# GEGLU feed-forward on one core: x's second half transposed in four places, stored by two transfers behind w_down's loads; the 21 staging steps spread anew; T3's second half later

## The chip, the cores and the metric

One core of one Trainium2 chip runs the kernel. The metric is the device time of one execution in microseconds (us); the time shown for a kernel is the median over several runs. Engines are named as the profile names them: PE is TensorE (matmuls; PEld are its weight loads), DVE is VectorE, ACT is ScalarE, POOL is GpSimd, and SPq and ACTq are the queues in which SyncE and ScalarE issue DMAs. Each engine and each queue works in the order of its program, so an instruction that waits holds everything behind it.

## The reference

With x of 2048 x 1024, w_gate and w_up of 1024 x 3584 and w_down of 3584 x 1024, all in bfloat16:

```python
def reference(x, w_gate, w_up, w_down):
    return (_gelu(x @ w_gate) * (x @ w_up)) @ w_down      # _gelu: tanh form
```

## The kernel before

**Seven products in place of eight.** Every matrix product is cut into 2 x 2 blocks and done with the seven products m1 to m7 of the Strassen-Winograd scheme. It needs sums of blocks on both sides. For the first two matmuls the sums of weights are s1 to s4 and a22 (`s_sum`: s1, s2, s4 on POOL, s3 on DVE in the stage in question (`s3_both`, L490), a22 on ACT), and the sums of the transposed x are t1, t2, t3, b22 and t4 (`t_sum`, L300 on DVE, b22 on ACT). For the third matmul the left sums come from the hidden activations (`s_down`, L763, DVE), and the right sums T1 to T4 from w_down. T2 and T4 of w_down are the same for all four output groups, so they are made once, early, and kept in DRAM (`t_dram`).

**Order of the work.** The 2048 rows of x are two halves `h` of 1024. For each half the kernel makes the hidden activations `hT` (28 tiles of 128 features by 1024 rows, "pairs" of tiles at a time), then multiplies by w_down in two groups (`down_group`). For h = 0 the sequence of pairs is: `first_units` (plain products of eight tiles, and the sums t1 to t4), the two pairs MID (4, 5), the eight pairs LEADS (0, 1, 2, 3, 6, 7, 8, 9), then two ordinary groups of two pairs, (10, 11) and (12, 13). For one pair, `quads` issues the products in the order m6/m5, then m7, m3, m4, each for gate (j = 0) and up (j = 1), of four matmuls each: 40 matmuls a pair. MID and the ordinary groups issue 32 plain matmuls ahead of their two pairs; LEADS do not, since theirs come from `first_units`. Between the products, DVE adds (`add_m5`, L527: PSUM bank plus the saved m5), ACT copies and applies the gelu (L313), and DVE multiplies gelu by up into hT (`mult`, L318). The third product m3 reads the bank that the first add writes, so PE waits for that add.

**Hooks.** The lists `thens` name, for each pair, what is issued at a point of its sequence: "start" (before its products), "m5" (after the first two adds), "m7", "m3" and "m4" (after those products), and "m1" (between the plain products of a group). All is put on engines and queues in this written order: `on` chains the instructions of each engine.

**Staging of w_down's sums.** `stage_load` (L701) loads two rows of blocks of w_down into one of three `wd_sb` buffers. `stage_step(n)` (L718 on DVE, 128 x 1024), n from 0 to 20, works in threes: the first makes a difference in a buffer of `o_sb`, the second subtracts it from another block in place and stores the buffer to `t_dram` (L721, 512 KB), the third makes the other sum in the other `o_sb` buffer and stores that as well. There are two such buffers, so a step that begins a buffer anew must wait until the last store from it has landed. `run_steps(n)` issues the next n steps; `run_loads` issues the loads that have become due. `run_late` issues one `s_down` "s3" on DVE. For the down phase itself, `load_wd_rows` (L633) fetches the first eight row blocks of w_down by two loads of 1 MB, issued on SPq at the m7 of pair 11; the buffers of pair 11's weights must be free by then.

**x's second half.** For h = 1 the transposed x is fetched in two parts. Its second 512 rows go into the buffer `xT1` by eight DMA transposes on SPq (`stage_x` with tb = 1, L214), two at the start of each of the third to sixth LEADS pairs. Its first 512 rows have no buffer yet: eight DMA transposes (L737) put them into tiles 24 to 27 of hT, which hold weights of chunk (0, 4) until the last LEADS pair's sums are made and get their activations in group (12, 13). `store_x` (L742) moves them from there to `x_dram`, and `x_fill` (L1125) loads them back in the down phase.

```python
        def run_x():
            m = 2 if xs[:1] and xs[0][0] == 1 else 4
            for q in xs[:m]:
                stage_x(hT, *q)
            del xs[:m]
```

Of the kernel before, what the change touches and what calls it, by code (L numbers as in the profile page):

```python
# [34 lines left out]
def kernel(  # L35
# [8 lines left out]
    nc = tc.nc  # L44
# [5 lines left out]
    KD = D // P  # L50
    KH = KD // 2
# [78 lines left out]
    def sp(inst):  # L130
        return on("sp", inst)
# [88 lines left out]
    def new_x(tb):  # L220
        xT[tb] = xT_pool.tile([P, KD, TB], BF16, name=f"xT{tb}")
# [147 lines left out]
    def first_units(hT):  # L369

        gs = {}

        def gelus(held, tiles):
            for u, t in enumerate(tiles):
                gs[t] = gelu(banks[held[u][0]])

        def outs(held, tiles):
            for u, t in enumerate(tiles):
                mult(hT, gs[t], banks[held[u][1]], t, 0)

        sets = ((VB, RB), (QB, PB), (QB, PB), (VB, RB))

        def top(n, j, k0, k1):
            tiles = (2 * n, 2 * n + 1)
            plain_products(sets[n], tiles, j, k0, k1)
            if k1 == KH:
                hold(sets[n], tiles, j)

        def rest(n):
            tiles = (2 * n, 2 * n + 1)  # L390
            plain_products(sets[n], tiles, 0, KH, KD)
            gelus(sets[n], tiles)
            plain_products(sets[n], tiles, 1, KH, KD)
            return sets[n], tiles

        transpose_x0(0)
        warm(RB[1], TB // 2)
        top(0, 0, 0, KPQ)
        top(0, 1, 0, KPQ)
        transpose_x0(1)  # L400
        top(1, 0, 0, KPQ)
        top(0, 0, KPQ, KH)
        top(0, 1, KPQ, KH)
        top(1, 1, 0, KPQ)
        top(1, 0, KPQ, KH)
        top(1, 1, KPQ, KH)
        outs(*rest(1))
        outs(*rest(0))
        for j in range(2):
            top(2, j, 0, KH)  # L410
        for j in range(2):
            top(3, j, 0, KH)
        t_sum("t1", 0, KH // 2)
        t_sum("t1", KH // 2, KH)
        t_sum("t2")
        outs(*rest(2))
        t_sum("t3", 0, KH // 2)
        t_sum("t3", KH // 2, KH)
        t_sum("b22")
        outs(*rest(3))  # L420
        t_sum("t4", 0, KH // 2)
        t_sum("t4", KH // 2, KH)
        for j in range(2):
            s_sum(0, MID[0], j, "s3")
        for j in range(2):
            for name in ("s1", "s2"):
                s_sum(0, MID[0], j, name)
        for j in range(2):
            s_sum(0, MID[0], j, "s4")
# [291 lines left out]
            sp(nc.sync.dma_start(out=dst, in_=t.bitcast(F32)))  # L721


    staged_x = []

    def x_rows(k0, k1):
        return x_dram[k0:k1, :, :].rearrange("k p t -> p k t")

    def stage_x(hT, tb, kd):
        if tb == 1:  # L730
            load_xT(xT, 1, tb, kd, kd + 1)
            return
        c0 = kd % NTB * TB
        f0 = KF - KD // NTB + kd // NTB
        t = hT[:, f0 : f0 + 1, c0 : c0 + TB]
        src = xv[SH : SH + TB, kd : kd + 1, :]
        sp(nc.sync.dma_start_transpose(out=t, in_=src))  # L737
        staged_x.append((x_rows(kd, kd + 1), t))

    def store_x():  # L740
        for dst, src in staged_x:
            sp(nc.sync.dma_start(out=dst, in_=src))  # L742
        staged_x.clear()

    def s_down(hT, grp, name, i0, i1):
        n = 0 if name in ("s1", "s2", "s4") else 1
# [223 lines left out]
    for h in range(NH):  # L970
# [33 lines left out]
                stage_load(loads.pop(0))  # L1004

        def run_x():
            m = 2 if xs[:1] and xs[0][0] == 1 else 4
            for q in xs[:m]:
                stage_x(hT, *q)
            del xs[:m]  # L1010

        if h == 0:
            run_loads()

            def load_half(c, f0):
                if f0 == 0:
                    new_chunk((0, c))
                for j in range(2):
                    load_w((0, c), j, 0, KD, act, f0, f0 + FA)

            thens = [
                {
                    "start": [
                        lambda j=j: s_sum(0, MID[0], j, "a22") for j in range(2)
                    ],
                    "m5": [lambda: load_half(3, 0)],
                    "m3": [lambda: run_steps(1)],
                    "m4": [lambda: new_x(1), run_loads],
                },
                {  # L1030
                    "m5": [lambda: load_half(3, FA)],
                    "m7": [lambda: fetch_to(QB, 0)],
                    "m3": [lambda: run_steps(1), run_loads],
                },
            ]
            quads(hT, h, MID, (h, LEADS[0]), thens, False, True, True)
            thens = [{} for _ in LEADS]
            for n in range(NL):
                thens[n]["start"] = []
                thens[n]["m3"] = [lambda: run_steps(1), run_loads]  # L1040
            for n in range(NL // 2):
                thens[2 + n]["start"].append(run_x)
            thens[1]["start"].append(lambda: load_half(4, 0))
            thens[3]["start"].append(lambda: load_half(4, FA))
            thens[5]["start"].append(lambda: load_half(5, 0))
            thens[5]["m7"] = [lambda: load_chunk((0, 6))]
            thens[7]["start"] += [lambda: load_half(5, FA), run_x]
            thens[7]["m3"].append(run_x)
            thens[7]["m4"] = [store_x]
            quads(hT, h, LEADS, (h, begin), thens, True, False, True)  # L1050
            s_late.append(
                shared_pool.tile([P, NL // 2 * TB], F32R, name="s_late")
            )
            run_late()

        for lead in range(begin, NPAIR, PPG):
            members = range(lead, lead + PPG)
            thens = [{} for _ in members]

            def add(n, name, *fs):  # L1060
                thens[n].setdefault(name, []).extend(fs)

            add(1, "m3", lambda key=(h, lead // PPG + 2): load_chunk(key))
            if h == 0:
                add(0, "m1", lambda: run_steps(2), run_loads)
                few = lead == NPAIR - PPG
                add(0, "start", lambda: run_steps(2), run_loads)
                for n in range(1 if few else PPG):
                    add(n, "m3", lambda: run_steps(1), run_loads)
                    add(n, "m4", run_late)  # L1070
            for n, pair in enumerate(members):
                if pair == NPAIR - 2 - (h == 0):
                    add(
                        n,
                        "start" if h else "m7",
                        lambda: load_wd_rows(0, 4),
                        lambda: load_wd_rows(4, 8),
                    )
                if h > 0 and 6 < pair < 11:
                    i = s3_late[pair - 7]  # L1080
                    at = "start" if n == 0 else "m3"
                    add(n, at, lambda i=i: s_down(hT, 0, "s3", i, i + 2))
                if pair < NPAIR - 1:
                    continue
                add(
                    0,
                    "m1",
                    lambda: early.append(wd_pool.tile([P, WDT, D], BF16, name="wd_sb")),
                    lambda: s_down(hT, 0, "s3", 0, 4),
                )  # L1090
                add(
                    n,
                    "start",
                    lambda: load_b22(4, NS),
                    lambda: load_wd_rows(8, 10),
                    lambda: load_wd_rows(10, 12),
                    lambda: load_wd_rows(12, NS),
                    lambda: load_b22(0, 4),
                )
                add(n, "m6", lambda: t_down(0, "t1", 4, 6))  # L1100
                add(n, "m7", lambda: s_down(hT, 0, "s1", 4, 8))
                add(n, "m7", lambda: s_down(hT, 0, "s1", 0, 4))
                add(n, "m3", lambda: t_down(0, "t1", 0, 2))
                add(
                    n,
                    "m4",
                    lambda: t_down(0, "t2", 0, NT2),
                    lambda: t_down(0, "t1", 2, 4),
                    lambda: t_down(0, "t1", 6, 8),
                    lambda: s_down(hT, 0, "s1", 8, NS),  # L1110
                    lambda: t_down(0, "t1", 8, NS),
                )
            nxt = (h, lead + PPG) if lead + PPG < NPAIR else None
            quads(hT, h, members, nxt, thens, lead == 0)
# [78 lines left out]
```

## Time and profile before

| what | value |
|---|---|
| median of 3 runs (range) | 548.77 us (548.61 to 550.17) |
| the profiled execution's own time | 549.52 us |
| its span, first to last instruction | 547.7 us |
| mean granted TensorE clock | 0.994 |
| PE busy | 535.0 us, 98% of the span |
| DVE busy | 379.9 us, 69% |
| ACT busy | 274.0 us, 50% |
| POOL busy | 254.9 us, 47% |
| moved by DMA | 102.70 MB, 188 GB/s on average |

The page gives busy time by engine, the span in 40 slices, the chain of work that ended last, groups of instructions by line, and DMA issues. A busy PE says little alone: matmuls are pipelined and their ends are modelled, so what counts is where PE stood idle and at which granted clock it ran. Where a time of day is given below, it counts from the start of the span.

### The profile page before, as it was taken

The page shows a single profiled execution, that of the slowest core. Times are in us where ns is not written, and L with a number is a line of the kernel's source. Part 1 is how long each engine was busy: PE and PEld are TensorE (multiplying, and loading weights), DVE is VectorE, ACT ScalarE, POOL GpSimd, SP SyncE. Part 2 cuts the span into 40 slices and gives each one's busy share as a digit, 9 for nine tenths or more (in the row PEclk, how much of TensorE's full clock was granted, in tenths as well). Part 3 has the DMA queues.
Part 4 walks back from the last instruction along what each step waited for, and adds up shares of the span by engine and source line. Part 5 has one row for each costly group of instructions (what it writes and reads, how often), then busy time and mean ns, then how long its engine had stood idle before and what let it go on. Part 6 is the DMA issues. An engine that isn't in the chain of part 4 may idle for free.

```text
span 547.7 us, 7014 instructions
## 1 busy us (share of the span) xinstructions
PE 535.0 (98%) x2380; PEld 383.8 (70%) x2380; DVE 379.9 (69%) x467; ACT 274.0 (50%) x471; POOL 254.9 (47%) x202
## 2 busy tenths in 40 slices
PE   9999999999599999999999999999999999999997
PEld 4448888886376767768668686867767686866866
DVE  1496899999479999789574352535444659979951
ACT  4456666665245416414565555555565552462270
POOL 0098999997546800000025594949586770000000
PEclk9999999999979999999999999999999999999999
DMA  8964357599766596969980404133140419677846
GB/s 235 264 229 117 115 177 170 161 262 222 240 193 230 186 350 231 332 204 328 298 278 0 154 1 156 32 122 92 62 152 3 153 60 330 230 251 245 287 145 204
DMA packets 97844, 102.70 MB, mean 188 GB/s; under 512 B 18320, under 2 KB 72720, under 8 KB 97808
## 3 DMA queue, kind: packets, MB, share of 16 engines
q1 hardware_dynamic: 71344, 82.52, 48.1%
q10 hardware_dynamic: 26464, 19.73, 12.0%
q8 instruction: 19, 0.31, 0.2%
q14 instruction: 17, 0.14, 0.1%
HBM read 85.98 MB, written 12.58 MB: 180 GB/s over the span
## 4 chain that ended last, share of the span: by engine, by line
PE 95%; DVE 2%; issue 1%; SPq 1%; DMA 1%; ACT 0%; DVEq 0%
PE bank L511 57%; PE bank L791 32%; PE bank L355 5%; DVE o_sb L718 1%; DVE hT L318 1%; SPq L742 1%; PE bank L245 1%; DMA t_dram<-o_sb 1%; PE bank L337 0%; DVE bank L527 0%; SPq L737 0%; ACT o_sb L847 0%; DVEq L718 0%; DVE wd_sb L763 0%; DVEq L318 0%
## 5 line engine op out<-in xcount | busy, mean ns | idle before, releaser
L511 PE MATMUL bank<-t_mem,s_mem 128*128 128x512 f32 x1096 | 254.6, 393 | 7.3 <-DVE bank L527 7.3
L511 PEld LDWEIGHTS bank<-t_mem,s_mem 128*128 128x128 f32 x1096 | 207.0, 189 | 52.2 <-issue 8.3
L462 POOL TENSOR_TENSOR s_mem<-w_mem 128x512 fp32r<-128x512 bf16 x80 | 101.0, 1281 | 186.0 <-DVE t_mem L300 94.8
L318 DVE TENSOR_TENSOR hT<-w_mem,bank 128x512 bf16<-128x512 f32 x106 | 71.1, 684 | 68.9 <-PE bank L511 40.3
L527 DVE TENSOR_TENSOR bank<-bank,m 128x512 f32<-128x512 f32 x112 | 72.3, 693 | 47.3 <-ACT m L567 45.1
L791 PE MATMUL bank<-t_mem,s_mem 128*128 128x512 f32 x416 | 98.1, 393 | 0.0
L313 ACT ACTIVATE w_mem<-bank 128x512 f32<-128x512 f32 x106 | 62.7, 597 | 65.8 <-DVE bank L527 44.6
L791 PEld LDWEIGHTS bank<-t_mem,s_mem 128*128 128x128 f32 x416 | 78.1, 188 | 17.1
L511 PE MATMUL bank<-xT,w_mem 128*128 128x512 bf16 x320 | 71.1, 379 | 0.9 <-DVE hT L318 0.9
L462 POOL TENSOR_TENSOR s_mem<-w_mem,s_mem 128x512 fp32r<-128x512 bf16 x46 | 65.1, 1434 | 7.9 <-PE bank L511 7.9
L690 DVE TENSOR_TENSOR t_mem<-w_mem 128x1024 fp32r<-128x1024 bf16 x56 | 66.7, 1240 | 0.4 <-PE bank L511 0.4
L511 PEld LDWEIGHTS <-w_mem 128*128 128x128 bf16 x320 | 30.6, 98 | 39.2 <-issue 3.8
L462 POOL TENSOR_TENSOR s_mem<-s_mem,w_mem 128x512 fp32r<-128x512 f32 x46 | 54.7, 1208 | 0.2
L572 ACT COPY bank<-bank 128x512 f32<-128x512 f32 x56 | 32.0, 572 | 23.3 <-PE bank L511 19.7
L567 ACT COPY m<-bank 128x512 f32<-128x512 f32 x56 | 33.0, 589 | 19.2 <-PE bank L511 19.1
L475 ACT CAST s_mem<-w_mem 128x512 fp32r<-128x512 bf16 x48 | 29.5, 616 | 25.6 <-PE bank L511 24.4
L791 PEld LDWEIGHTS <-hT 128*128 128x128 bf16 x224 | 21.3, 98 | 26.6 <-issue 2.1
L856 ACT CAST o_sb<-bank 128x512 bf16<-128x512 f32 x27 | 14.9, 586 | 33.7 <-PE bank L791 33.7
L791 PE MATMUL bank<-t_mem,s_late 128*128 128x512 f32 (+1 forms) x132 | 30.3, 382 | 0.0
L537 ACT COPY bank<-bank 128x512 f32<-128x512 f32 x40 | 22.8, 570 | 13.2 <-PE bank L511 13.2
L763 DVE TENSOR_TENSOR s_mem<-hT 128x512 fp32r<-128x512 bf16 x36 | 23.6, 688 | 6.4 <-PE bank L791 6.4
L791 PEld LDWEIGHTS bank<-t_mem,s_late 128*128 128x128 f32 x132 | 24.4, 188 | 4.9
(61 smaller groups left out, 400.8 us busy)
## 6 DMA issues: line engine op xcount, KB each, us to landing
t_mem<-t_dram SPq DMA_DIRECT2D x56, 512.0 KB, 5.2
wd_sb<-in_w_down_dram SPq DMA_DIRECT2D x26, 512.0 KB, 6.9
t_dram<-o_sb SPq DMA_DIRECT2D x14, 512.0 KB, 3.3
w_mem<-in_w_gate_dram ACTq DMA_DIRECT2D x6, 1024.0 KB, 5.8
w_mem<-in_w_up_dram ACTq DMA_DIRECT2D x6, 1024.0 KB, 8.2
w_mem<-in_w_gate_dram SPq DMA_DIRECT2D x8, 512.0 KB, 6.1
w_mem<-in_w_up_dram SPq DMA_DIRECT2D x8, 512.0 KB, 7.1
w_mem<-in_w_down_dram SPq DMA_DIRECT2D x4, 1024.0 KB, 7.2
```

The source lines that it names most:

```text
L313: act(nc.scalar.activation(out=g_sb, in_=ps[:], func=ACT.Gelu_apprx_tanh))
L318: nc.vector.tensor_tensor(out=hT[:, fc, tb * TB : (tb + 1) * TB], in0=g_sb, in1=ps[:], op=ALU.mult,)
L355: nc.tensor.matmul(banks[held[u][j]][:], lhsT=w_sb[:, kd, f0 : f0 + P], rhs=xT[0][:, kd, :], start=kd == 0, stop=kd in (KH - 1, KD - 1), s ...
L462: pool(nc.gpsimd.tensor_tensor(out=t, in0=in0, in1=in1, op=op))
L475: act(nc.scalar.copy(out=t, in_=a(1, 1)))
L511: nc.tensor.matmul(banks[bank][:], lhsT=lhs[:, c, :], rhs=rhs[:, c, :], start=start and c == 0, stop=c == KH - 1, skip_group_check=True,)
L527: nc.vector.tensor_tensor(out=banks[dst][:], in0=banks[src][:], in1=m5[:], op=ALU.add)
L567: act(nc.scalar.copy(out=m5[j][:], in_=banks[V_[j]][:]))
L572: act(nc.scalar.copy(out=banks[R_[j]][:], in_=banks[Q_[j]][:]))
L690: dve(nc.vector.tensor_tensor(out=t, in0=in0, in1=in1, op=ALU.subtract))
L763: dve(nc.vector.tensor_tensor(out=t, in0=in0, in1=in1, op=op))
L791: nc.tensor.matmul(banks[bank][:, c0:c1], lhsT=lhs(i, u), rhs=rhs(i)[:, c0:c1], start=start and i == 0, stop=stop and i == NS - 1, skip_gr ...
```

## The change

Five things change; the matmuls, the sums and every value computed stay the same.

1. In `first_units`, the second half of t3 is issued on DVE behind the multiplications of the last plain unit and behind b22, instead of ahead of them.
2. The 21 staging steps are spread anew. Before: one step at the m3 of each MID pair and of each LEADS pair (steps 0 to 9), then six in group (10, 11) and five in group (12, 13): two at "m1", two at "start", one at the m3 of each pair but the very last. Now: the first MID pair takes three (start, m3, m4), the second one; LEADS take one each, the last of them at its m4 instead of its m3; the two groups take two at "m1", one at "start" and one at each m3, as long as there are any (steps 12 to 16 and 17 to 20).
3. The eight transposes into hT, before four at the start and four at the m3 of the last LEADS pair, are issued two at its start, two at its m7, two at its m3 and two at its m4.
4. `store_x`, before eight stores of 128 KB at the m4 of the last LEADS pair, becomes two stores of 512 KB: one at the m5 of pair 10, one at its m3, each behind a load of w_down in SPq.
5. One more `run_late` at the m4 of pair 10, so that the late "s3" sums end sooner.

```diff
         t_sum("t3", 0, KH // 2)
-        t_sum("t3", KH // 2, KH)
         t_sum("b22")
         outs(*rest(3))
+        t_sum("t3", KH // 2, KH)
...
-        staged_x.append((x_rows(kd, kd + 1), t))
-
-    def store_x():
-        for dst, src in staged_x:
-            sp(nc.sync.dma_start(out=dst, in_=src))
-        staged_x.clear()
+
+    def store_x(hT, k0, k1):
+        f0 = KF - KD // NTB
+        t = hT[:, f0 + k0 // NTB : f0 + k1 // NTB, :]
+        src = t.rearrange("p a (b c) -> p (a b) c", b=NTB)
+        sp(nc.sync.dma_start(out=x_rows(k0, k1), in_=src))
...
         def run_x():
-            m = 2 if xs[:1] and xs[0][0] == 1 else 4
-            for q in xs[:m]:
+            for q in xs[:2]:
                 stage_x(hT, *q)
-            del xs[:m]
+            del xs[:2]
...
                     "start": [
-                        lambda j=j: s_sum(0, MID[0], j, "a22") for j in range(2)
+                        lambda: s_sum(0, MID[0], 0, "a22"),
+                        lambda: s_sum(0, MID[0], 1, "a22"),
+                        lambda: run_steps(1),
                     ],
                     "m5": [lambda: load_half(3, 0)],
                     "m3": [lambda: run_steps(1)],
-                    "m4": [lambda: new_x(1), run_loads],
+                    "m4": [lambda: new_x(1), lambda: run_steps(1), run_loads],
...
             thens[7]["start"] += [lambda: load_half(5, FA), run_x]
-            thens[7]["m3"].append(run_x)
-            thens[7]["m4"] = [store_x]
+            thens[7]["m4"] = thens[7]["m3"] + [run_x]
+            thens[7]["m7"], thens[7]["m3"] = [run_x], [run_x]
...
                 add(0, "m1", lambda: run_steps(2), run_loads)
-                few = lead == NPAIR - PPG
-                add(0, "start", lambda: run_steps(2), run_loads)
-                for n in range(1 if few else PPG):
+                add(0, "start", lambda: run_steps(1), run_loads)
+                for n in range(PPG):
                     add(n, "m3", lambda: run_steps(1), run_loads)
                     add(n, "m4", run_late)
+                if lead == begin:
+                    add(0, "m5", lambda: store_x(hT0, 0, KH))
+                    add(0, "m3", lambda: store_x(hT0, KH, KD))
+                    add(0, "m4", run_late)
```

More of the change, by code (lines that the diff above doesn't have):

```diff
@@ L721, in stage_step @@
             sp(nc.sync.dma_start(out=dst, in_=t.bitcast(F32)))
-    staged_x = []
     def x_rows(k0, k1):
```

## The prediction

> **What bounds the kernel now.** I read the chain of work that ended last, in order of time, then the waits of PE, then the timeline and SPq around the one long gap, and last the stretches around it. PE carries 95% of the chain, and its waits are few:
>
> ```profile
> PE bank L511 <- DVE bank L527: 7.3, 2, 6.9
> PE bank L511 <- DVE hT L318: 0.9, 2, 0.5
> ```
>
> (Total, times, longest.) So all that can be won short of fewer matmuls is one wait of 6.9 us, three of 0.4 to 0.5, and what follows from them. The chain shows where the 6.9 comes from; the timeline shows the same place by engine:
>
> ```profile
> 139.89 4.28 SPq L742 DMA_DIRECT2D x_dram<-hT  x8
> ...
> 144.28 0.93 SPq L721 DMA_DIRECT2D t_dram<-o_sb  x2
> ...
> 147.22 1.76 DVE L718 TENSOR_TENSOR o_sb<-wd_sb 128x1024 fp32r<-128x1024 bf16 x1 [7.00 <-DMA t_dram<-o_sb]
> 149.01 2.06 DVE L718 TENSOR_TENSOR o_sb<-wd_sb,o_sb 128x1024 fp32r<-128x1024 bf16 x1
> 150.99 2.48 DVE L527 TENSOR_TENSOR bank<-bank,m 128x512 f32<-128x512 f32 x4
> ...
> 151.82 4.55 PE L511 MATMUL bank<-t_mem,s_mem 128*128 128x512 f32 x10 [6.90 <-DVE bank L527]
> ```
>
> Steps 10 and 11 ended at 137.9, but their stores sat in SPq behind four transposes and the eight stores of x until 144.28. Step 12 begins the buffer that step 10 stored, so DVE stood 7.00 us, then did steps 12 and 13, and only then the adds for which pair 10's m3 waited. The stretches show a second price:
>
> ```profile
> core 0: us, PE busy (x) PEld busy (x) DVE busy (x) ACT busy (x) POOL busy (x), PEclk, DMA share, GB/s
> ...
> 145.00:151.82 6.82, 0.00 (x1) 0.03 (x1) 4.57 (x4) 0.00 (x0) 4.98 (x4) 0.82 0.69 236
> 151.82:156.20 4.38, 4.38 (x10) 3.45 (x11) 2.86 (x5) 1.19 (x2) 1.65 (x2) 0.50 0.76 239
> ```
>
> Behind the gap the granted clock was 0.50 until about 156.2. Elsewhere the chain has 412 matmuls in 93.37 us, 0.227 each; ten should take 2.27 and took 4.55, so the ramp costs 2.28.
>
> **The parts.**
>
> *Stores of x* (parts 3 and 4). In the changed program's order, no store of x stands ahead of a staging store that DVE will soon need: the first is behind the store of step 14 and a load, the second behind a load that waits for step 15. What had to be late is step 10's store; it now comes ahead of all hT transposes (step 10 is at the seventh LEADS pair's m3, where step 8 is now; the store that goes there, at 125.27, lands at 130.8); step 12 needs it at about 136. Removed: 6.90 of idling and the ramp of 2.28, together 9.2. Matmul ends are modelled: the 24 ahead of the gap have 5.84 us where 24 x 0.227 is 5.44, so up to 0.4 more may be idling; I take 0.2.
>
> What is late next is step 11's store, behind six transposes. These start at 126.24 as now; the first took 2.54 and the others about 1.21 in the rows, so the sixth has been issued at 135.1. Step 11, now behind the last LEADS pair's last multiplication, ends near 134.5, so its store goes at 135.1 and lands at 137.8 to 141.5 (L721's rows: 2.7, 3.3 and 6.4 at least, median and most). Step 14 waits for it: ahead of it on DVE are one late sum, steps 12 and 13 and the second plain multiplication, now ending at 140.2 with its PE wait, some 0.4 earlier then: 139.8. Its adds can't begin before their m5 copies, now 142.8, then 142.4. With POOL idle until 142.3, a step takes 1.22, so landing by 141.1 costs nothing, and 141.5 costs 0.4 on DVE. I take 0. The two x stores are two issues of 0.4 (L721's rows of 512 KB) in place of eight of 0.45; nothing waits for them until pairs 12 and 13 write hT, near 164 on the new clock, over 10 us later.
>
> *LEADS to group (10, 11).* PE's wait of 0.43 at 134.95 is for the last LEADS multiplication (134.22), held by step 9 (132.18, 2.12 us). With the last step behind that multiplication it can run at its product's end: 0.4 won.
>
> *t3's half.* The wait of 0.47 at 36.74 is for a multiplication that ran at 35.42, after both t3 halves (31.32, 4.17 us). With one half ahead, it runs when PE has finished, near 34.2: 0.5 won. The half itself (2.1) and t4 (36.62, 4.32) then end near 41.3 in place of 40.9; t3 is needed by m7 at 44.5, t4 by m4 at 48.1, less the 0.5.
>
> *More steps in MID.* Step 0 falls in DVE's idle 2.50 us ahead of 44.62: free. Step 2, at the first pair's m4, takes 2.13 where DVE had 1.29 us:
>
> ```profile
> 51.73 0.67 DVE L318 TENSOR_TENSOR hT<-w_mem,bank 128x512 bf16<-128x512 f32 x1
> ...
> 52.49 0.57 ACT L572 COPY bank<-bank 128x512 f32<-128x512 f32 x1 [0.61 <-DVE hT L318]
> 53.07 0.59 ACT L567 COPY m<-bank 128x512 f32<-128x512 f32 x1
> 53.12 2.29 POOL L462 TENSOR_TENSOR s_mem<-w_mem 128x512 fp32r<-128x512 bf16 x2 [0.27 <-PE bank L511]
> 53.69 0.70 DVE L527 TENSOR_TENSOR bank<-bank,m 128x512 f32<-128x512 f32 x1 [1.29 <-ACT m L567]
> ```
>
> Queued behind it are the adds, a sum and, at the end of the second pair, the multiplication that frees the bank for ACT's copy ahead of m7. That multiplication, at 61.5 now, comes 0.8 to 1.7 late (the second, if one more DVE operation is held 0.9 by POOL). It may come 0.9 late before PE waits (copy of 0.57, m7 of up at 63.5), 0.4 with PE 0.5 earlier. So 0 to 1.3 is lost here; I take 0.4. From then on each LEADS pair has as much DVE work as now, and the first has 1.5 us of DVE idling to catch up in.
>
> *Group (12, 13).* "start" has one step in place of two, so adds that began at 178.76 and held PE for 0.42 could begin 1 to 2 us sooner. Against it, step 18 now stands ahead of the plain multiplications and waits for step 16's store. SPq has that store behind two 1 MB loads of w_down; it is issued near 157.4 on the new clock, while the second load (10.8 us in its row) is still in flight, and lands after 3.3 to 6.4, which is 0 to 3 us too late for step 18. The two together: 0.4 won to 0.5 lost; I take 0.2 won. The extra run_late (0.7 to 1.0) meets a DVE idle of 1.61 at 161.1: nothing.
>
> **Sum.** Won 9.2 + 0.2 + 0.4 + 0.5 + 0.2 - 0.4 = 10.1. The profiled execution took 549.52 (span 547.7), so the same execution would take 539.4. It was 0.75 above the median of its runs, 548.77; the median goes to 538.7. With each term at its ends (modelled ends 0 to 0.4, t3 and MID +0.5 to -0.8, group (12, 13) +0.4 to -0.5, step 11's store 0 to 0.4 lost), 10.9 to 7.9 are won: 537.9 to 540.9.
>
> One rule bears on the ramp. The Trainium skill ("TensorE: Matmul & The Clock Gate", Part 1) says that the clock falls to half after an idle window of about 3.4 us and returns after as long of work; the trace agrees at 6.9 us idle (half clock for 4.4) and at 0.4 to 0.5 (no fall), and has no gap between. By that rule a leftover gap just under 3.4 us would cost itself alone, so 2.28 more of the gain would stay than by a ramp in proportion.
>
> **Rivals.**
>
> *A. The wait moves to step 14.* If the six transposes are each as slow as the first (2.54), step 11's store goes at 141.5 and lands at 144.2 to 147.9; step 14 and the first add take 1.22 and 0.7, and m3 is due at 144.1. PE then waits 2 to 5.7, with a ramp at the upper end: 541 to 547, say 543.5. For it: the first transpose did take 2.54 and its batch landed late. Against: seven of eight issues took 1.1 to 1.3. Chance 0.08.
>
> *B. The wait moves to step 18.* If step 16's store lands as slowly as the load ahead of it (10.8), near 168, step 18 is 7 late, and the copy ahead of m7 in pair 12 with it: PE waits about 5 and ramps, 7.5 in all: 546.5. Half of that is likelier: 542.5. Against it: the x stores have left, and loads issued since are no longer than now. Chance 0.08.
>
> *C. Slower: DVE and POOL hold each other through LEADS.* A step takes 2.13 there and 1.22 while POOL is idle, and POOL's sums 1.17 or 2.15. From 60 to 130 us DVE is busy 63.80 of 70 and POOL 67.90. If the new phase of DVE (later by up to 1.7) makes one more operation of each wait 0.91 in every pair, a pair's 9.07 us grow by 1.82 less POOL's idle 0.29, eight times: 12.2 lost, 10.1 won, 550.9. It decides from 1.2 us lost a pair. Against it: the order of work inside a LEADS pair is unchanged, and the first one has DVE idling in which the lag ends. Chance 0.06.
>
> The Trainium skill ("SBUF — State Buffer", Who interferes with whom) speaks for C: a DVE instruction with two SBUF inputs and a POOL instruction that reads SBUF exclude each other, and whichever issues first blocks the other for its whole length. The trace agrees with 1.22 against 2.13. By the rule a step put where POOL works costs one of them about 0.9, as the upper end for MID has it already.
>
> *D. It doesn't do what it says:* a wait of the same length stays, for a store at another place or since SPq was not its cause: 548 to 549. Against it: 144.28, the moment the x stores end, is when the store goes. Chance 0.04.
>
> **Numbers.** My case has 0.74. Faster: it with A and B, 0.90; within 0.3% (1.65 us, about what a measurement of this kernel can tell from no change): D, 0.04; slower: C, 0.06. The range of 8 in 10 takes in my case's own ends, 0.2 below for the scatter of runs (548.61 to 548.77 for the lower two), and the likelier parts of A and B: 537.7 to 543.5.
>
> **What would show it.** Right: no DVE wait for t_dram<-o_sb near 140, PE's longest wait under 1 us, granted clock 1.00 from 130 to 190, x stores near 143 and 149 with nothing waiting, span near 538. Step by step: PE waits at 36.7, 135 and 179 gone; a new one of up to 1 near 63. A would show a DVE wait ahead of step 14, B one ahead of step 18, C PE waits at each m7 in LEADS. Wrong: any PE gap over 2 us, or a LEADS pair longer than 9.1.

## The result, and the profile after

The changed kernel takes 540.96 us (median of 4 runs, 540.88 to 541.42) beside 549.11 for the kernel before on the same chip (4 runs): a ratio of 0.985, 95% interval 0.983 to 0.987. Its profiled execution took 540.88 with a span of 539.1 and a mean granted clock of 1.000.

The waits of PE (engine, line, what it waited for: total, times, longest, in us):

```profile
PE bank L511 <- ACT bank L572: 0.9, 1, 0.9
...
PE bank L511 <- DVE hT L318: 0.2, 1, 0.2
```

The line for `DVE bank L527` (7.3 in all) is gone, and so are two waits of 0.4 to 0.5 for L318. A wait of 0.9 for an ACT copy is new. The timeline shows the staging steps, SPq and the place of the old gap (start, length, engine, line, operation, count, and in brackets what the engine waited for):

```profile
126.15 9.20 SPq L735 DMA_TRANSPOSE hT<-in_x_dram  x6
...
135.44 0.53 SPq L721 DMA_DIRECT2D t_dram<-o_sb  x1
...
138.90 18.51 PE L511 MATMUL bank<-t_mem,s_mem 128*128 128x512 f32 x80
...
139.97 1.22 DVE L718 TENSOR_TENSOR o_sb<-wd_sb,o_sb 128x1024 fp32r<-128x1024 bf16 x1
...
142.70 1.40 SPq L741 DMA_DIRECT2D x_dram<-hT  x1
```

PE now runs from 138.90 for 18.51 us without a stop, through the place where it stood for 6.90 us. Step 11's store goes at 135.44, and step 14 begins at 139.97 with no wait in brackets. The first x store goes at 142.70, the second at 149.35, and nothing waits for either. The same two stretches as before, with the columns of the prediction's table:

```profile
145.00:151.82 6.82, 6.82 (x32) 5.64 (x31) 6.33 (x7) 4.45 (x8) 6.82 (x6) 1.00 0.86 279
151.82:156.20 4.38, 4.38 (x21) 3.64 (x20) 3.87 (x7) 1.79 (x3) 4.38 (x4) 1.00 1.04 353
```

PE is busy in all of both and the granted clock is 1.00; the second holds 21 matmuls where it held 10.

The new wait, in the timeline of the changed kernel:

```profile
67.27 3.30 POOL L462 TENSOR_TENSOR s_mem<-hT,s_mem 128x512 fp32r<-128x512 bf16 x2
...
70.60 0.38 ACTq L203 DMA_DIRECT2D hT<-in_w_up_dram  x1
71.07 0.59 ACT L567 COPY m<-bank 128x512 f32<-128x512 f32 x1 [2.64 <-POOL s_mem L462]
71.55 1.08 ACT L572 COPY bank<-bank 128x512 f32<-128x512 f32 x2
...
72.20 2.11 PE L511 MATMUL bank<-t_mem,s_mem 128*128 128x512 f32 x8 [0.89 <-ACT bank L572]
```

ScalarE issues `load_half(4, 0)` at the start of the second LEADS pair. The load overwrites weights that POOL's s4 still reads until 70.57, so it goes at 70.60, and ACT, whose copies are queued behind it, stands for 2.64. The first of the two L572 copies fills the bank that m7 then adds to, and PE starts at 72.20. DVE's multiplication, for which the second copy waited before (71.53, 0.19 us), was done at 70.13.

### The profile page after: what moved, and what is told of

Same layout as the page of the kernel before. It is cut to its first block, busy times and chain, and to the rows that moved or that the text cites. A ratio compares the mean times of both kernels' runs of the same rounds, so it can differ in the third digit from the quotient of the medians.

```text
span 539.1 us, 6990 instructions
## 1 busy us (share of the span) xinstructions
PE 531.2 (99%) x2360; PEld 381.7 (71%) x2380; DVE 376.5 (70%) x467; ACT 273.6 (51%) x471; POOL 255.2 (47%) x202
## 4 chain that ended last, share of the span: by engine, by line
PE 94%; POOL 2%; issue 2%; DMA 1%; DVE 0%; SPq 0%; ACT 0%; ACTq 0%; DVEq 0%
PE bank L511 56%; PE bank L789 33%; PE bank L355 5%; POOL s_mem L462 2%; DMA hT<-in_w_gate_dram 1%; SPq L209 0%; DVE wd_sb L761 0%; DVE hT L318 0%; ACT bank L572 0%; SPq L203 0%; ACTq L203 0%; ACT o_sb L845 0%; ACT m L567 0%; DVEq L318 0%; ACTq L572 0%
## 5 line engine op out<-in xcount | busy, mean ns | idle before, releaser
L462 POOL TENSOR_TENSOR s_mem<-w_mem 128x512 fp32r<-128x512 bf16 x80 | 99.6, 1263 | 180.5 <-DVE t_mem L300 95.2
L318 DVE TENSOR_TENSOR hT<-w_mem,bank 128x512 bf16<-128x512 f32 x106 | 71.1, 684 | 69.2 <-PE bank L511 39.7
L527 DVE TENSOR_TENSOR bank<-bank,m 128x512 f32<-128x512 f32 x112 | 72.5, 694 | 46.2 <-ACT m L567 41.9
L462 POOL TENSOR_TENSOR s_mem<-s_mem,w_mem 128x512 fp32r<-128x512 f32 x46 | 55.8, 1235 | 0.2
L572 ACT COPY bank<-bank 128x512 f32<-128x512 f32 x56 | 31.9, 572 | 24.4 <-PE bank L511 19.7
```

The costliest lines, as they stand in the source:

```text
L318: nc.vector.tensor_tensor(out=hT[:, fc, tb * TB : (tb + 1) * TB], in0=g_sb, in1=ps[:], op=ALU.mult,)
L462: pool(nc.gpsimd.tensor_tensor(out=t, in0=in0, in1=in1, op=op))
L527: nc.vector.tensor_tensor(out=banks[dst][:], in0=banks[src][:], in1=m5[:], op=ALU.add)
L572: act(nc.scalar.copy(out=banks[R_[j]][:], in_=banks[Q_[j]][:]))
```

## The experiments

Times are medians, the ratio is to the kernel before on the same chip, and each edit is against the kernel named.

**Where the long gap went: size, place and spread.** First the two large stores at the old place (against before):

```diff
...
-            thens[7]["m4"] = [store_x]
+            thens[7]["m4"] = [
+                lambda: store_x(hT0, 0, KH),
+                lambda: store_x(hT0, KH, KD),
+            ]
```

> The kernel before with only the number of x's stores changed: two of 512 KB in place of eight of 128 KB, at the same place. Theory: SPq then spends 1 to 2 us on them in place of 4.3, waits for the last transposes to land (141.2), and step 10's store goes near 142; step 12's wait falls from 7.0 to 4.5 to 5, PE's from 6.9 to about 4.7, still with the ramp: 546.5 to 547. If the 512 KB stores held the stores behind them by their own length, nothing is won or time is lost: 548 to 550.

Measured: 548.47 us (10 runs, 547.44 to 550.38), ratio 0.9995 [0.9981, 1.0008]: no difference that these runs can tell, where 546.5 to 547 was expected. The timeline:

```profile
141.03 1.83 SPq L721 DMA_DIRECT2D t_dram<-o_sb  x2
...
146.06 1.24 DVE L718 TENSOR_TENSOR o_sb<-wd_sb 128x1024 fp32r<-128x1024 bf16 x1 [6.41 <-DMA t_dram<-o_sb]
...
150.14 6.07 PE L511 MATMUL bank<-t_mem,s_mem 128*128 128x512 f32 x15 [5.80 <-DVE bank L527]
```

Step 10's store now leaves SPq at 141.03 in place of 144.28, 3.25 sooner, but step 12 starts only 1.16 sooner (146.06 for 147.22): it begins 5.0 us after the store's issue in place of 2.9, with x's megabyte issued just ahead. PE's gap shrinks by 1.10 and the half clock behind it stays.

Then the place alone: the two large stores where the change has them, everything else as before (against before):

```diff
...
-            thens[7]["m4"] = [store_x]
...
+                if lead == begin:
+                    add(0, "m5", lambda: store_x(hT0, 0, KH))
+                    add(0, "m3", lambda: store_x(hT0, KH, KD))
```

> The kernel before with one part of the change alone: x goes to DRAM by two stores of 512 KB at the m5 and the m3 of pair 10, while the transposes (four and four), the 21 steps and t3 stay as before. Theory (the SPq order made the long wait, step 10's store behind the x stores): that store now has only four transposes ahead, is issued at 139.9 in place of 144.28 and lands near 143; step 12 waits for it some 2.5 us in place of 7.0, and PE's wait of 6.9 falls to 2 to 3. If a wait this short leaves the clock at 1.00, 2.3 more are saved: 4.1 + 2.3, about 542.7; with a ramp 545. Rival (the wait is not due to SPq): PE's wait stays at 6 to 7 and the time at 548 to 549.

Measured: 544.13 us (543.77 to 544.89), ratio 0.9912 [0.9897, 0.9927], a little over half of the gain. The timeline and the stretches:

```profile
142.71 1.52 DVE L718 TENSOR_TENSOR o_sb<-wd_sb 128x1024 fp32r<-128x1024 bf16 x1 [2.79 <-DMA t_dram<-o_sb]
...
147.08 11.21 PE L511 MATMUL bank<-t_mem,s_mem 128*128 128x512 f32 x42 [2.47 <-DVE bank L527]
```

```profile
143.30:146.60 3.30, 1.31 (x6) 0.75 (x4) 3.27 (x3) 0.12 (x1) 3.30 (x2) 1.00 0.58 194
146.70:150.00 3.30, 2.92 (x7) 2.37 (x8) 2.71 (x5) 1.20 (x2) 3.30 (x4) 0.50 0.86 232
150.10:153.00 2.90, 2.90 (x14) 2.34 (x14) 2.35 (x3) 1.49 (x3) 2.90 (x3) 1.00 0.77 273
```

With the x stores away, step 10's store still stands behind eight transposes until 139.62, and DVE waits 2.79 for it; PE waits 2.47. Behind this shorter gap the clock is at half as well (0.50 in the second row): seven matmuls in 3.07 us in place of 1.59, so the ramp costs 1.48 more. The rest of the gain must come from the other parts.

Then the spread without the place: the changed kernel with eight stores of 128 KB at the last LEADS pair's m4 again (against the changed kernel):

```diff
...
-            thens[7]["m4"] = thens[7]["m3"] + [run_x]
+            thens[7]["m4"] = thens[7]["m3"] + [run_x, store_x]
...
-                    add(0, "m5", lambda: store_x(hT0, 0, KH))
-                    add(0, "m3", lambda: store_x(hT0, KH, KD))
```

> The changed kernel with x stored as before: eight stores of 128 KB at the m4 of the last LEADS pair, behind the last transposes. The steps stay spread, so step 10's and step 11's stores are ahead of the x stores; step 13's store comes behind them, near 144, and lands near 147, when step 15 wants it (147.2). Theory (the order of the staging stores decides, not the number or place of the x stores): no DVE wait over 0.5 us, 541 give or take 0.5. Rival (the place and size of the x stores decide): a DVE wait of several us returns and PE waits 3 to 7 us near 145, 544 to 550.

Measured: 541.28 us (540.90 to 542.17), ratio 0.9861 [0.9846, 0.9876], the time of the whole change.

```profile
135.15 0.53 SPq L721 DMA_DIRECT2D t_dram<-o_sb  x1
...
139.76 3.83 SPq L742 DMA_DIRECT2D x_dram<-hT  x8
139.89 1.22 DVE L718 TENSOR_TENSOR o_sb<-wd_sb,o_sb 128x1024 fp32r<-128x1024 bf16 x1
```

The eight stores hold SPq until 143.6, as they did before, but the store that DVE needs next (step 11's, 135.15) is ahead of them, and step 14 runs at 139.89 without a wait. The new spread of the steps is enough without the large late stores of x, which add nothing that these runs can tell. This kernel also has parts 1 and 5 and the transposes in four places; the spread was not tried without them.

**t3's half** (against the changed kernel):

```diff
+        t_sum("t3", KH // 2, KH)
         t_sum("b22")
         outs(*rest(3))
-        t_sum("t3", KH // 2, KH)
```

> The changed kernel with t3's second half where it was, ahead of the last plain multiplications. Theory: PE's wait of 0.47 near 36.7 comes back, with 0.15 of restart, and nothing else moves: 0.6 slower than the changed kernel, 541.5. Rival (the half was hidden anyway, or the later half costs as much in the MID pairs): no difference beyond 0.2, or faster, with PE's wait in the second LEADS pair smaller by as much.

Measured: 541.25 us (541.07 to 541.64), ratio 0.9859 [0.9844, 0.9874], 0.3 above the changed kernel's 540.96 and inside the scatter. (This t3 is the sum of the transposed x; the title writes it T3.) The copy that ACT makes of the product behind the wait shows what the order costs PE, first in this kernel, then in the changed one:

```profile
37.93 0.57 ACT L537 COPY bank<-bank 128x512 f32<-128x512 f32 x1 [0.47 <-PE bank L511]
```

```profile
37.04 0.57 ACT L537 COPY bank<-bank 128x512 f32<-128x512 f32 x1 [0.24 <-PE bank L511]
```

ACT waits 0.23 longer for PE with the old order here. With the two stores at the old place, which has the old order as well, it is 0.33; in the profile before 0.63; with the place alone 0; all profiles with the new order have the 0.24. It goes with the length of t3's first half: 1.68, 1.78, 2.08 and 1.22 us in these four. So the old order costs 0 to 0.6 us, by the execution, and the 0.47 that PE waited in the profile before is the most of the four.

**The two waits that are left.** The changed kernel once more, for comparison on the chip of the next three:

> The changed kernel unaltered, beside the next three on the same chip. 541.0, PE's waits of 0.89 in the second LEADS pair and 0.16 at pair 12 again, and a second look at the end of the span: 4.6 us between ScalarE's last copy and the span's end in the changed kernel's profile against 3.6 before. If that end belongs to the change it is 4.4 or more again; if it is scatter of the last stores' landing, it lies anywhere from 3.5 to 4.6.

Measured: 541.30 us (540.61 to 541.63), ratio 0.9857 [0.9840, 0.9874]; PE waits 1.15 for L572 at 72.47 and 0.16 at pair 12, and the end of the span takes 4.5 us again.

ACT's load later (against the changed kernel):

```diff
-            thens[1]["start"].append(lambda: load_half(4, 0))
+            thens[1]["m5"] = [lambda: load_half(4, 0)]
```

> The changed kernel with one ScalarE load moved: the first half of chunk (0, 4) is issued at the m5 of the second LEADS pair in place of its start. Theory (PE's wait of 0.89 there arises because ACT's queue holds this load until POOL has made the last s4, which comes late since the steps now in MID keep POOL from working, and ACT's copies for m5 and m7 stand behind it): that wait falls below 0.1, and the time by 1.0 to 1.2, to about 539.9. Rival (DVE's lag out of MID holds the copy, as the prediction had it): the wait stays near 0.9 and the time at 541.

Measured: 540.88 us (539.69 to 541.51), ratio 0.9848 [0.9829, 0.9868].

```profile
71.18 0.57 ACT L572 COPY bank<-bank 128x512 f32<-128x512 f32 x1 [0.28 <-PE bank L511]
...
72.23 0.37 ACTq L203 DMA_DIRECT2D hT<-in_w_gate_dram  x1
```

The copies go ahead of the load, wait for PE alone, and PE's wait is gone. Matched by ACT's instructions with the profile of the changed kernel, this one started 0.77 us later, was 0.45 ahead behind this place, 1.22 in all, and ended 0.41 ahead. So the trace shows the wait's whole price won; by the medians alone 0.4 us is inside the scatter.

The loads of w_down later, behind step 16's store (against the changed kernel):

```diff
-                        "start" if h else "m7",
+                        "start" if h else "m4",
```

> The changed kernel with the two 1 MB loads of w_down's first rows moved from pair 11's m7 to its m4, so that step 16's store is ahead of them in SPq. Theory (step 18 waits because that store shares the DMA engines with those loads, landing after 5.0 us where 2.7 to 3.3 are usual): it lands 3 us after its issue, DVE's gap of 1.5 ahead of step 18 falls below 0.3, PE's restart losses at pair 12 (0.6 in all) go, 540.4. Rival (step 18's chain is hidden or the adds bound it): no difference beyond 0.2. If the rows then come late for the down phase: slower.

Measured: 542.04 us (540.90 to 542.85), ratio 0.9872 [0.9853, 0.9891]. Of PE's waits only those for L572 (0.87 at 72.66) and the first of the program are left; that in group (12, 13) is gone. Step 16's store landed 3.1 us after its issue, and step 18 began at 161.71 with no wait. Yet nothing was won:

```profile
163.70 3.23 DVE L761 TENSOR_TENSOR wd_sb<-hT 128x512 fp32r<-128x512 bf16 x2
```

These two sums behind step 18 took 2.25 in the changed kernel. The adds of pair 12 began 0.48 later than there, and this profile had been 0.49 behind ahead of the place as well (matched by ACT's instructions). So the rival holds: taking step 18's wait away brings nothing. Another 0.18 were lost at 201, where the down phase begins; why stays open.

Both edits together, in two series:

> The changed kernel with both moves, the ScalarE load at the second LEADS pair's m5 and w_down's rows at pair 11's m4. If the two waits are independent the savings add: 1.1 + 0.6, 539.3; PE then has no wait over 0.2 behind its start. If one takes the place of the other, no better than the better of the two.

> The changed kernel with two more edits: load_half(4, 0) goes from the start of the second LEADS pair to its m5, and the two loads of load_wd_rows go from pair 11's m7 to its m4. Theory (each of PE's two leftover waits has one cause that its edit takes away): PE has no wait over 0.2 us at 72 and none over 0.35 at 167; the two were worth 1.16 + 0.4 = 1.5 us of PE's time in the changed kernel's own trace, so 541.1 - 1.5 = 539.6, between 539.2 and 540.4. Rival (waits of this size are made up elsewhere, by whatever comes next): between 540.9 and 541.4, with a new wait of 0.5 to 1 us somewhere in the trace.

Measured: 540.06 us (four runs; the fifth, which was the profiled one, took 1109.98 and is left out), ratio 0.9833 [0.9817, 0.9850]; then 539.62 us (539.22 to 540.48), ratio 0.9824 [0.9807, 0.9842]. In the second profile (span 537.4) the waits of PE have one line left, the first instruction of the program:

```profile
PE bank L245 <- PEq L1179: 0.8, 1, 0.8
```

These nine runs lie between 539.22 and 540.48, the eight of the changed kernel between 540.61 and 541.63: the version with both edits is the fastest here, by 0.9 to 1.7 of the medians. Matched by ACT's instructions with the changed kernel's profile, the second profile was 0.56 ahead from the start of the program, 1.77 ahead behind the place at 72, and 1.75 behind pair 12. So what the edits won, 1.2, is the load's; the rows' move won nothing here either.

**Is step 2 the cause of POOL's lag?** One step fewer at the first MID pair's m4, one more at the second's (against the changed kernel):

```diff
-                    "m4": [lambda: new_x(1), lambda: run_steps(1), run_loads],
+                    "m4": [lambda: new_x(1), run_loads],
...
                     "m3": [lambda: run_steps(1), run_loads],
+                    "m4": [lambda: run_steps(1), run_loads],
```

> The changed kernel with one staging step fewer at the first MID pair's m4 and one more at the second MID pair's m4; all else as it is. Theory (the new wait near 72 comes from POOL, which step 2 at the first MID pair's m4 put late): POOL's s1 in the second MID pair takes 2.3 in place of 2.97, its s4 in the first LEADS pair ends 0.6 to 0.8 sooner, at 69.8 to 70.0, ACT's load and the copies behind it go as much sooner, and PE's wait near 72 is at most 0.4. Against that, step 3 now stands ahead of the first LEADS pair's adds, 2.13 later for them, which may hold that pair's m3 by 0 to 0.6. In all 540.3 to 541.2. Rival (any step more in MID puts POOL late, wherever it is): the wait near 72 stays at 0.8 to 1.2, and 541.3 to 541.9.

Measured: 541.27 us (540.86 to 541.64), ratio 0.9848 [0.9831, 0.9865]. POOL's sums and what follows from them:

```profile
52.68 2.29 POOL L462 TENSOR_TENSOR s_mem<-w_mem 128x512 fp32r<-128x512 bf16 x2 [0.28 <-PE bank L511]
...
61.43 3.27 POOL L462 TENSOR_TENSOR s_mem<-w_mem 128x512 fp32r<-128x512 bf16 x2
```

```profile
72.83 3.47 PE L511 MATMUL bank<-t_mem,s_mem 128*128 128x512 f32 x14 [1.20 <-ACT bank L572]
```

The s1 pair at 52 took 2.29 in place of 2.97, as the theory had it, but the next one, at 61.43, took 3.27 in place of 2.29, ACT's load went at 71.23 in place of 70.60, and PE waited 1.20. (This profile was 0.32 behind the changed kernel's from the start.) The theory of this one step falls, and its rival holds: with four steps in MID, POOL is late at the first LEADS pairs, at whichever of these two m4 the step is put.

All three edits together:

> The edits of e9_both_again and of e10_step_moved together. Theory (POOL's lag costs only by ACT's load, which no longer waits for it): the same time as e9_both_again, 539.3 to 540.3, or up to 0.5 more if the first LEADS pair's m3 is held by step 3. Rival (POOL's lag costs something of its own in LEADS): 0.5 or more below e9_both_again.

Measured: 541.02 us (540.65 to 542.13), ratio 0.9847 [0.9829, 0.9866], 1.4 above the 539.62 of the same series without the step's move. The wait at 72 is absent, and one two pairs on has come, at the next load, `load_half(4, FA)`:

```profile
89.39 0.37 ACTq L203 DMA_DIRECT2D hT<-in_w_up_dram  x1
89.86 0.59 ACT L567 COPY m<-bank 128x512 f32<-128x512 f32 x1 [2.79 <-POOL s_mem L462]
...
90.99 2.34 PE L511 MATMUL bank<-t_mem,s_mem 128*128 128x512 f32 x9 [1.04 <-ACT bank L572]
```

The same chain, with the same copies behind a load that POOL holds. So POOL's lag costs where ACT's queue has a load that waits for POOL, and it lasts for pairs.

## Why the prediction was right, and by how much it was off

The sign, the place and the mechanism of the main term were right, and 540.96 is in the range of 537.7 to 543.5. The forecast of 538.7 was 2.26 us too low. By PE's steps in the two traces (one matmul's start to the next, less 0.227):

| term | predicted | measured |
|---|---|---|
| stores of x: gap and ramp, with modelled ends | +9.2 +0.2 | +7.07 +2.11 = 9.18 |
| LEADS to group (10, 11) | +0.4 | +0.58 |
| t3's half | +0.5 | +0.63 |
| more steps in MID | -0.4 | -1.16 |
| group (12, 13) | +0.2 | +0.17 |
| the start of the program | 0 | +0.13 |
| the end of the program | 0 | -0.90 |
| sum, by the two profiled executions | 10.1 | 8.63 |

- *The stores of x* held step by step: store of step 11 at 135.44 (forecast 135.1), landed at 138.97 (137.8 to 141.5), step 14 at 139.97 (139.8). But it credited parts 3 and 4 together; two of the runs show that the spread of the steps does it without the stores' place, and that this place alone wins a little over half.
- *More steps in MID* is the term whose mechanism failed; that 1.16 lies in its bounds of 0 to 1.3 is luck. The wait was looked for near 63, at the multiplication that came late there; ACT's copy behind that one was 0.1 late, and PE did not wait. The step that failed was "From then on each LEADS pair has as much DVE work as now, and the first has 1.5 us of DVE idling to catch up in". DVE did catch up (its multiplication at 69.45 was on time). POOL didn't: its s1 pair behind the added step took 2.97 in place of 2.29, and its s2 pair in the first LEADS pair 3.27 in place of 2.30 (before, then after):

```profile
64.22 2.30 POOL L462 TENSOR_TENSOR s_mem<-s_mem,hT 128x512 fp32r<-128x512 f32 x2
```

```profile
64.03 3.27 POOL L462 TENSOR_TENSOR s_mem<-s_mem,hT 128x512 fp32r<-128x512 f32 x2
```

  DVE's s3 beside the second took 1.57 in place of 2.12: before, DVE was held longer there, now POOL is. The Trainium skill ("SBUF — State Buffer", Who interferes with whom) has the lock that fits this, and the prediction used it only for DVE and for rival C. Then what was queued behind POOL was missed: ACT's load, and behind that the copy that fills m7's bank.
- *Group (12, 13)*: the sum came out, but not for the reasons given. The wait of 0.42 at 179.59 is gone, and step 18 waits for step 16's store (issued at 157.56 for 157.4, landed 5.0 us later):

```profile
162.67 1.74 DVE L718 TENSOR_TENSOR o_sb<-wd_sb 128x1024 fp32r<-128x1024 bf16 x1 [1.48 <-issue]
...
167.23 4.99 PE L511 MATMUL bank<-t_mem,s_mem 128*128 128x512 f32 x20 [0.16 <-DVE hT L318]
```

  With that wait taken away (the loads of w_down later) nothing was won, so it isn't what the losing half of the term is made of.
- *t3's half* was right for the two profiles and too large for the kernel: the old order costs 0 to 0.6 in four profiles. The largest of them was booked as one that all have.
- *The end of the program* was no term at all. From the start of ScalarE's last copy to the span's end it took 3.7 us before and 4.6 after; the last store of SyncE landed 2.1 us after its issue, then 2.9. The three profiles with the old spread have 3.2 to 3.7, the nine with a new spread 4.2 to 4.6. What the stores meet there stays open.
- *The offset.* 0.75 was taken off because the profiled execution was that much above the median of three runs. The changed kernel's profiled execution lies 0.08 below its own median, so 0.83 of the miss is here; the rest is the sum's 1.5. With more runs, the median before is 549.1 to 549.7 in four series.

Of the rivals, A did not come (six transposes took 9.20, and step 14 didn't wait); B came at 1.48 on DVE and 0.16 on PE, not 5; C did not: PE waits nowhere between 73 and 132; D falls with the result. (B's sum was off: 538.7 and 7.5 are 546.2, not 546.5.) "PE's longest wait under 1 us" held at 0.89 in this profile, not in the kernel's second, at 1.15.

The Trainium skill's rule on the clock ("TensorE: Matmul & The Clock Gate", Part 1), as the prediction cites it, was taken to mean that a gap under 3.4 us has no ramp. The gap of 2.47, with the place alone, had one of 1.48 us.

## What to carry to other kernels

When a store stands behind others in a queue, look first at which store the waiting engine needs next: issuing that one earlier was enough, while making the others larger or later brought nothing more. When a step is added beside a shared engine, follow the lag of the other engine as well, to the queue that holds a load until it is done: work behind that load waits as well. And before a small wait of one profile is booked as a gain, see whether a second execution has it as long.

## What the runs showed of the hardware

The granted clock fell and returned at steps of about 3.4 us. Before, it is half in two such stretches:

```profile
145.90:149.30 3.40, 0.00 (x0) 0.00 (x0) 2.05 (x2) 0.00 (x0) 3.40 (x3) 1.00 0.97 316
149.40:152.70 3.30, 0.88 (x2) 0.82 (x3) 3.30 (x4) 0.00 (x0) 0.58 (x1) 0.50 0.38 143
152.80:156.10 3.30, 3.30 (x9) 2.62 (x8) 1.78 (x4) 1.19 (x2) 1.55 (x2) 0.50 0.75 225
```

With the place alone it is half in one, and the stretch that brought the fall was not idle: PE was busy for 1.31 of its 3.30 us. The stretch behind the fall had PE busy for 2.92 of 3.30 there, and the clock came back at its end; before, with 0.88 of 3.30, it took one stretch more (1.00 from 156.20). The Trainium skill ("TensorE: Matmul & The Clock Gate", Part 1) has a free-running window of 3413 ns; the lengths agree. It speaks of an idle window, and that does not: a window with PE busy for four tenths was enough here. What came behind a gap was 1.48 us after one of 2.47, 2.11 after one of 6.90, and 2.51 after one of 5.80 (the two stores at the old place, where the clock was half from 148.5 to 155.3). It does not go with the length of the gap alone: from the gap's end to the clock's return it was 3.0, 4.4 and 5.2 us, and about half of each was lost. How it goes with where a gap falls among the windows was not tried by itself.
